# RetNet attention and a two-layer MLP: weight conversion rebuilt over three engines, raw loads on the sync queue, decay factors applied before the transposes

## The chip, the cores and the metric

One core of a Trainium2 chip. The metric is device microseconds of one execution; lower is better. Every kernel here was run four to five times beside runs of the kernel before on the same chip. Medians are given with their range. A ratio is the mean time of one kernel's runs over the mean of the other's in the same rounds, so it is not quite the ratio of the medians that stand beside it.

## The reference, cut to what matters

```python
# q, k, v: (8, 8, 576, 64) float32      8 batches, 8 heads, 576 positions
scores = (1 / np.sqrt(64)) * np.matmul(q, k.transpose(0, 1, 3, 2))
gamma = 1.0 - 2.0 ** (-5.0 - np.arange(8))
Dmat = np.where(rel >= 0, gamma[:, None, None] ** rel, 0.0)   # rel = row - column
ret = np.matmul(scores * Dmat, v)
x = ret.transpose(0, 2, 1, 3).reshape(4608, 512)
# moe_w_in (512, 2048) and moe_w_out (2048, 512) arrive as float64, alpha as float32
h = x @ w_in
g = np.maximum(h, 0.0) + alpha * np.minimum(h, 0.0)
out = g @ w_out
```

The kernel must turn the float64 weights into float32 itself. It reads each as two 32-bit words and works on 32 pieces of 128x512 weights.

## The kernel before: the parts that matter

Attention is done in 16 couples (one batch, four heads); the MLP in 192 units (384 tokens, 128 hidden columns), each with a first half (`ph`, four matmuls with w_in) and a second half (`po`, three matmuls with w_out); the traces show each of these matmuls as two records, so 8 and 6. The first eight pieces of weights are issued with couple 0, the next eight with couple 1, and so on up to couple 3. A scheduler then fixes each engine's order of instructions, and the engines run ahead of each other as far as buffers and waits allow (in the trace before, GpSimd starts its last scaling of k at 941.6 us, and TensorE the last matmul that reads it at 1066.2). In these kernels the results of the matmuls are tiles in PSUM; the copies and products by which another engine takes them out of there are called evictions below.

One piece of weights. `a` and `b` have two buffers each, `raw` too:

```python
def load_weights(n):
    for _ in range(min(n, len(pieces))):
        ...
        raw = wraw.tile([P, FQ, 2], INT32, tag="raw", name=f"raw_{at}")
        nc.gpsimd.dma_start(raw, src.rearrange("p (n two) -> p n two", two=2))
        lo = raw[:, :, 0].bitcast(UINT32)
        hi = raw[:, :, 1].bitcast(FP32)
        ...
        nc.gpsimd.tensor_scalar(a, hi, HI_MAX, -HI_MAX, ALU.min, ALU.max)          # clamp
        nc.gpsimd.tensor_tensor(out=b, in0=a, in1=a, op=ALU.mult)                  # square
        nc.vector.scalar_tensor_tensor(out=a, in0=b, scalar=HI_MIN * HI_MIN, in1=a,
                                       op0=ALU.is_ge, op1=ALU.mult)                # threshold
        nc.vector.tensor_scalar(bi, ai, 3, 0x3FFFFFF8,
                                ALU.logical_shift_left, ALU.bitwise_and)
        nc.vector.scalar_tensor_tensor(out=bi, in0=ai, scalar=-0x40000000, in1=bi,
                                       op0=ALU.bitwise_and, op1=ALU.bitwise_or)
        nc.vector.tensor_scalar(ai, bi, -0x00800000, None, ALU.bitwise_and)
        nc.vector.scalar_tensor_tensor(out=a, in0=lo, scalar=2.0 ** -52, in1=a,
                                       op0=ALU.mult, op1=ALU.mult)
        nc.gpsimd.tensor_tensor(out=dst, in0=a, in1=b, op=ALU.add)
```

The decay: k is scaled on GpSimd before its transpose, q by a table on VectorE after it:

```python
def transposes(n, b, u, tiles):
    ...
    nc.gpsimd.tensor_tensor(out=kr, in0=kr, in1=krem[...], op=ALU.mult)
    for j in range(NJ):
        nc.gpsimd.tensor_tensor(out=kn[:, j], in0=kn[:, j], in1=ktab[...], op=ALU.mult)
    for i in range(2):
        ...  # four transposes of qn into pt
        nc.vector.tensor_tensor(out=qT[i], in0=pt, in1=qtab[...], op=ALU.mult)
    ...      # rT: a product and a copy, both on VectorE
    for i in range(2):
        ...  # four transposes of kn into pt
        nc.scalar.copy(kT[i], pt)
```

## Time and profile before

| kernel before | |
|---|---|
| median of four runs | 1276.91 us (1276.35 to 1280.6) |
| span of the profiled run | 1276.2 us |
| first and last weight piece finished | 27.65 and 250.36 us |
| TensorE busy in the first 260 us | 197.9 us |
| TensorE's work at the full clock (worked out in the prediction) | 1165 us, and 9.1 us of output behind it |

The table of windows in slices of 40 us shows the conversion stage at a glance. Columns: stretch, length, busy us of PE, PEld, DVE, ACT, POOL with the number of instructions, then granted TensorE clock, DMA share, GB/s.

```profile
0.00:40.00 40.00, 23.40 (x195) 19.59 (x195) 23.86 (x59) 7.33 (x20) 23.44 (x115) 0.91 0.84 192
80.00:120.00 40.00, 31.27 (x197) 19.87 (x196) 30.80 (x55) 3.55 (x8) 26.58 (x32) 0.91 0.58 142
200.00:240.00 40.00, 29.02 (x160) 17.20 (x159) 27.61 (x50) 1.93 (x4) 25.46 (x29) 0.84 0.43 120
```

In these stretches TensorE has 9 to 17 us of gaps in 40, and its clock is not 1.00 either. From 256 us on it is full. ScalarE is nearly idle, while VectorE and GpSimd together are busy for 47 to 57 us of each 40.

### The profile page before, as it was taken

Reading aid. Unit: us, or ns where it says so; the run is one execution under the profiler, and the core shown is the slowest. Engines: PE = TensorE matmul, PEld = TensorE weight load, DVE = VectorE, ACT = ScalarE, POOL = GpSimd, SP = SyncE. Lnnn points to the kernel's source line nnn. Section 1 sums busy time; section 2 is a strip of 40 time slices with the busy share of each in tenths; the row PEclk is TensorE's granted clock in tenths of the full one; section 3 lists DMA queues with packets and bytes.
Section 4 is the critical chain, followed back from the end, with each engine's and each line's share of the span. In section 5 each row is a group of like instructions: output and inputs, shape, how many; then the busy total and the mean of one; then the engine's idle time right before and its main releaser. Section 6 shows DMA issues by size and latency. Waiting matters only on the chain.

```text
span 1276.2 us, 11815 instructions
## 1 busy us (share of the span) xinstructions
PE 1204.7 (94%) x4897; PEld 676.0 (53%) x4897; DVE 448.2 (35%) x852; ACT 63.7 (5%) x129; POOL 195.0 (15%) x337
## 2 busy tenths in 40 slices
PE   5788887899999999999999999999999999999997
PEld 4554344455555555555555655555555555555553
DVE  5778667522222323231232323231232323222221
ACT  1100000000000000000000000000000000000000
POOL 6666556500000100000000100000000000000000
PEclk8888898899999999999999999999999999999999
DMA  8754343200000201100100211100100000000000
GB/s 184 173 125 122 99 122 101 86 9 1 25 0 1 60 21 36 45 17 18 46 17 19 63 40 35 46 17 19 46 17 19 25 1 1 25 1 1 25 1 25
DMA packets 122773, 55.30 MB, mean 43 GB/s; under 512 B 116304, under 2 KB 116320, under 8 KB 122720
## 3 DMA queue, kind: packets, MB, share of 16 engines
q1 hardware_dynamic: 115200, 28.33, 10.2%
q0 software_dynamic: 7520, 26.23, 6.3%
q8 instruction: 38, 0.62, 0.2%
q14 instruction: 15, 0.12, 0.0%
HBM read 45.10 MB, written 9.44 MB: 43 GB/s over the span
## 4 chain that ended last, share of the span: by engine, by line
PE 56%; issue 27%; DVE 5%; POOL 5%; DMA 5%; SPq 1%; POOLq 0%
PE po L225 25%; PE ph L240 25%; DMA raw<-in_moe_w_in_dram 3%; PE ps L304 2%; DMA raw<-in_moe_w_out_dram 2%; DVE wa L209 1%; POOL wb L198 1%; DVE wb L205 1%; PE pv L349 1%; POOL w_in L211 1%; POOL wa L197 1%; POOL w_out L211 1%; PE pv L358 1%; SPq L75 1%; PE pu L327 1%
## 5 line engine op out<-in xcount | busy, mean ns | idle before, releaser
L240 PE MATMUL ph<-xT,w_in 128*128 128x384 f32 x1536 | 545.5, 494 | 12.5 <-POOL w_in L211 12.5
L225 PE MATMUL po<-w_out,g 128*128 128x512 f32 x1152 | 536.4, 601 | 10.7 <-POOL w_out L211 8.3
L240 PEld LDWEIGHTS ph<-xT,w_in 128*128 128x128 f32 x1536 | 287.7, 192 | 234.6 <-issue 76.7
L244 DVE TENSOR_SCALAR neg<-ph,alpha 128x384 f32<-128x384 f32 x192 | 118.3, 617 | 679.8 <-PE ph L240 679.4
L225 PEld LDWEIGHTS po<-w_out,g 128*128 128x128 f32 x1152 | 220.5, 193 | 247.7 <-issue 189.2
L233 POOL DMA_DIRECT2D out_dram<-osb x36 | 20.0, 555 | 738.5 <-ACT osb L231 738.4
L246 DVE SCALAR_TENSOR_TENSOR g<-ph,neg 128x384 f32<-128x384 f32 x192 | 106.8, 557 | 6.1
L265 POOL TENSOR_TENSOR kn<-kn,ktab 128x256 f32<-128x256 f32 x64 | 43.7, 698 | 171.1 <-DMA kn<-in_k_dram 170.9
L304 PE MATMUL ps<-qT,kT 64*128 64x128 f32 x512 | 52.3, 296 | 11.4 <-DVE at L308 7.7
L304 PEld LDWEIGHTS ps<-qT,kT 64*128 64x128 f32 x512 | 45.2, 198 | 28.3 <-DVE at L308 12.0
L308 DVE TENSOR_TENSOR at<-ps,mask 128x512 f32<-128x512 f32 x64 | 41.9, 684 | 32.8 <-PE ps L304 32.8
L361 ACT COPY xT<-pv 128x512 f32<-128x512 f32 x32 | 18.4, 587 | 519.7 <-PE pv L358 518.7
L199 DVE SCALAR_TENSOR_TENSOR wa<-wb,wa 128x512 f32<-128x512 f32 x32 | 25.1, 786 | 40.9 <-POOL wb L198 40.8
L231 ACT COPY osb<-po 128x512 f32<-128x512 f32 x36 | 21.1, 586 | 305.8 <-PE po L225 273.4
L293 ACT COPY kT<-ptk 128x512 f32<-128x512 f32 x32 | 17.6, 588 | 368.5 <-PE ptk L290 368.5
L349 PEld LDWEIGHTS pv<-at,vn 128*64 128x64 f32 x512 | 30.6, 147 | 9.8 <-issue 8.1
L198 POOL TENSOR_TENSOR wb<-wa 128x512 f32<-128x512 f32 x32 | 34.2, 1070 | 2.2
L349 PE MATMUL pv<-at,vn 128*64 128x128 f32 x512 | 34.3, 289 | 0.0
L358 PE MATMUL pv<-qT,sums 128*128 128x128 f32 x192 | 27.2, 286 | 2.6 <-DVE sums L337 2.6
L337 DVE TENSOR_TENSOR sums<-pu,sums 64x128 f32<-64x128 f32 x96 | 27.7, 289 | 3.0
L197 POOL TENSOR_SCALAR wa<-raw 128x512 f32<-128x512 f32 x32 | 22.4, 699 | 39.9 <-DMA raw<-in_moe_w_in_dram 26.3
L205 DVE SCALAR_TENSOR_TENSOR wb<-wa,wb 128x512 int32<-128x512 int32 x32 | 27.7, 864 | 0.5
(58 smaller groups left out, 406.2 us busy)
## 6 DMA issues: line engine op xcount, KB each, us to landing
out_dram<-osb POOLq DMA_DIRECT2D x36, 256.0 KB, 2.4
qn<-in_q_dram SPq DMA_DIRECT2D x64, 128.0 KB, 3.1
kn<-in_k_dram SPq DMA_DIRECT2D x64, 128.0 KB, 3.0
raw<-in_moe_w_in_dram POOLq DMA_DIRECT2D x16, 512.0 KB, 4.2
vn<-in_v_dram SPq DMA_DIRECT2D x64, 128.0 KB, 3.0
raw<-in_moe_w_out_dram POOLq DMA_DIRECT2D x16, 512.0 KB, 3.8
qr<-in_q_dram SPq DMA_DIRECT2D x32, 32.0 KB, 3.2
kr<-in_k_dram SPq DMA_DIRECT2D x32, 32.0 KB, 2.6
```

The lines of the kernel that those rows point to most:

```text
L197: nc.gpsimd.tensor_scalar(a, hi, HI_MAX, -HI_MAX, ALU.min, ALU.max)
L198: nc.gpsimd.tensor_tensor(out=b, in0=a, in1=a, op=ALU.mult)
L205: nc.vector.scalar_tensor_tensor(out=bi, in0=ai, scalar=-0x40000000, in1=bi, op0=ALU.bitwise_and, op1=ALU.bitwise_or)
L225: nc.tensor.matmul(acc[kb][m], g[:, m * P:(m + 1) * P], w_out[fc // FCQ][:, fc % FCQ, :], start=(fc == 0), stop=(fc == NFC - 1))
L240: nc.tensor.matmul(ph, w_in[fc // FCQ][:, cc, f0:f0 + P], xT[grp][:, cc, t0:t0 + TB], start=(cc == 0), stop=(cc == NCC - 1))
L244: nc.vector.tensor_scalar(neg, ph, 0.0, alpha[:, fc:fc + 1], ALU.min, ALU.mult)
L246: nc.vector.scalar_tensor_tensor(out=g, in0=ph, scalar=0.0, in1=neg, op0=ALU.max, op1=ALU.add)
L265: nc.gpsimd.tensor_tensor(out=kn[:, j], in0=kn[:, j], in1=ktab[:, j, 4 * u:4 * u + 4, None].to_broadcast([P, 4, D]), op=ALU.mult)
L304: nc.tensor.matmul(ps[h2][:, cols], kT[i][rows, cols], qT[i][rows, cols], start=True, stop=True)
L308: nc.vector.tensor_tensor(out=a, in0=ps[h2].rearrange("p (j w) -> p j w", w=C), in1=mask[:, None, :].to_broadcast([P, NJ, C]), op=ALU.mult)
L349: nc.tensor.matmul(pv[i][h2 * D:(h2 + 1) * D, j * C:(j + 1) * C], vn[:, j, 2 * i + h2, :], at[2 * i + h2][:, j, :], start=(j == 0), stop=F ...
L358: nc.tensor.matmul(pv[i][:, j * C:(j + 1) * C], sm[:, j - 1, i, :], qT[i][:, j * C:(j + 1) * C], start=False, stop=(j == NJ - 1), skip_gro ...
```

## The change

The intent: fewer operations per weight piece on VectorE and GpSimd, with two of them on ScalarE; raw loads that do not stand in GpSimd's queue; one kind of scaling for q and k.

```diff
-            raw = wraw.tile([P, FQ, 2], INT32, tag="raw", name=f"raw_{at}")
-            nc.gpsimd.dma_start(raw, src.rearrange("p (n two) -> p n two", two=2))
+            raw = wraw.tile([P, FQ, 2], INT32, tag="raw", bufs=3, name=f"raw_{at}")
+            nc.sync.dma_start(raw, src.rearrange("p (n two) -> p n two", two=2))
...
             nc.gpsimd.tensor_scalar(a, hi, HI_MAX, -HI_MAX, ALU.min, ALU.max)
-            nc.gpsimd.tensor_tensor(out=b, in0=a, in1=a, op=ALU.mult)
+            nc.scalar.activation(l, lo, ACTF.Copy, scale=2.0 ** -29)
+            nc.scalar.activation(b, a, ACTF.Square)
...     # threshold, shift and merge stay on VectorE
-            nc.vector.tensor_scalar(ai, bi, -0x00800000, None, ALU.bitwise_and)
-            nc.vector.scalar_tensor_tensor(out=a, in0=lo, scalar=2.0 ** -52, in1=a,
-                                           op0=ALU.mult, op1=ALU.mult)
-            nc.gpsimd.tensor_tensor(out=dst, in0=a, in1=b, op=ALU.add)
+            nc.gpsimd.tensor_tensor(out=dst.bitcast(INT32), in0=bi, in1=l, op=ALU.add)
...     # transposes(): q and k in one tile, both scaled on GpSimd
+        for x in range(2):
+            for j in range(NJ):
+                nc.gpsimd.tensor_tensor(out=qk[:, x, j], in0=qk[:, x, j],
+                                        in1=tab[...], op=ALU.mult)
...
-            nc.vector.tensor_tensor(out=qT[i], in0=pt, in1=qtab[...], op=ALU.mult)
...     # rT as one copy on ScalarE; of the four transposed tiles
+                if i == 0:
+                    nc.vector.tensor_copy(dst[i], pt)
+                else:
+                    nc.scalar.copy(dst[i], pt)
```

Left out: a constant of the threshold step (`HI_MIN`), which the new operations need, and the small tables of decay factors. These are now built by repeated products on VectorE, from constants that VectorE and GpSimd set, in the first 10 us, where the kernel before used exponentials on ScalarE and a large table for q.

More of the change, by code (lines that the diff above doesn't have):

```diff
@@ L69, in load_couple @@
     def load_couple(b, u):
-        tiles = []
-        for name, src in (("q", q), ("k", k), ("v", v)):
-            t = nat.tile([P, NJ, 4, D], FP32, tag=f"nat_{name}", name=f"{name}n_{b}_{u}")
-            r = nat.tile([P, 2, D], FP32, tag=f"rem_{name}", name=f"{name}r_{b}_{u}")
+        qk = nat.tile([P, 2, NJ, 4, D], FP32, tag="nat_qk", name=f"qk_{b}_{u}")
+        qkr = nat.tile([P, 2, 2, D], FP32, tag="rem_qk", name=f"qkr_{b}_{u}")
+        vn = nat.tile([P, NJ, 4, D], FP32, tag="nat_v", name=f"vn_{b}_{u}")
+        vr = nat.tile([P, 2, D], FP32, tag="rem_v", name=f"vr_{b}_{u}")
+        for t, r, src in ((qk[:, 0], qkr[:, 0], q), (qk[:, 1], qkr[:, 1], k), (vn, vr, v)):
             for j in range(NJ):
@@ L82, in load_couple @@
                     src[b, h:h + 2, NJ * C:S, :].rearrange("h p d -> p h d"))
-            tiles += [t, r]
-        return tiles
+        return qk, qkr, vn, vr
     loaded = {0: load_couple(*couples[0]), 1: load_couple(*couples[1])}
@@ L89 @@
     make_identity(nc, ident)
-    lng = [float(np.log1p(-(2.0 ** (-5.0 - h)))) for h in range(H)]
-    wrow = const.tile([P, C], FP32, name="wrow")
-    nc.gpsimd.iota(wrow, pattern=[[1, C]], base=0, channel_multiplier=0,
-                   allow_small_or_imprecise_dtypes=True)
-    prow = const.tile([P, 1], FP32, name="prow")
-    nc.gpsimd.iota(prow, pattern=[[1, 1]], base=0, channel_multiplier=1,
-                   allow_small_or_imprecise_dtypes=True)
+    gam = [1.0 - 2.0 ** (-5.0 - h) for h in range(H)]
@@ new lines @@
+    NBIT = 7
+    pint = const.tile([P, 1], INT32, name="pint")
+    nc.gpsimd.iota(pint, pattern=[[1, 1]], base=0, channel_multiplier=1)
+    pbit = const.tile([P, NBIT], FP32, name="pbit")
+    pbi = const.tile([P, NBIT], INT32, name="pbi")
+    for i in range(NBIT):
+        nc.vector.tensor_scalar(pbi[:, i:i + 1], pint, i, 1,
+                                ALU.logical_shift_right, ALU.bitwise_and)
+    nc.vector.tensor_copy(pbit, pbi)
+    fac = const.tile([P, 2, NJ, H], FP32, name="fac")
@@ new lines @@
+    facr = const.tile([P, 2, NC2, 2], FP32, name="facr")
+    gpw = const.tile([P, NBIT, H], FP32, name="gpw")
+    for h in range(H):
+        for i in range(NBIT):
+            nc.gpsimd.memset(gpw[:, i, h:h + 1], float(np.float32(gam[h] ** 2 ** i)) - 1.0)
+    for h in range(H):
+        for j in range(NJ):
+            nc.vector.memset(fac[:, 0, j, h:h + 1], gam[h] ** (j * C - MID) / np.sqrt(D))
+            nc.vector.memset(fac[:, 1, j, h:h + 1], gam[h] ** (MID - j * C))
+    for u in range(NC2):
+        for i in range(2):
+            for h2 in range(2):
+                g_ = gam[4 * u + 2 * i + h2]
+                rows = slice(i * REM, (i + 1) * REM)
+                at_ = NJ * C - i * REM - MID
+                nc.gpsimd.memset(facr[rows, 0, u, h2:h2 + 1], g_ ** at_ / np.sqrt(D))
+                nc.gpsimd.memset(facr[rows, 1, u, h2:h2 + 1], g_ ** -at_)
@@ new lines @@
+    pw = const.tile([P, 2, H], FP32, name="pw")
+    pwt = const.tile([P, H], FP32, name="pwt")
+    for i in range(NBIT):
+        t_ = pw[:, 0, :] if i == 0 else pwt
+        nc.vector.tensor_scalar(t_, gpw[:, i, :], pbit[:, i:i + 1], 1.0, ALU.mult, ALU.add)
+        if i:
+            nc.vector.tensor_tensor(out=pw[:, 0, :], in0=pw[:, 0, :], in1=pwt, op=ALU.mult)
+    nc.vector.reciprocal(pw[:, 1, :], pw[:, 0, :])
+    tab = const.tile([P, 2, NJ, H], FP32, name="tab")
+    tabr = const.tile([P, 2, NC2, 2], FP32, name="tabr")
@@ L101 @@
+    for x in range(2):
+        nc.vector.tensor_tensor(out=tab[:, x], in0=fac[:, x],
+                                in1=pw[:, x:x + 1, :].to_broadcast([P, NJ, H]), op=ALU.mult)
+        for i in range(2):
+            rows = slice(i * REM, (i + 1) * REM)
+            nc.vector.tensor_tensor(
+                out=tabr[rows, x], in0=facr[rows, x],
+                in1=pw[rows, x].rearrange("p (u i h) -> p u i h", u=NC2, i=2)[:, :, i, :],
+                op=ALU.mult)
     mask = const.tile([P, C], FP32, name="mask")
@@ L107 @@
     nc.vector.memset(maskr[0:REM, REM:C], 0.0)
-    ktab = const.tile([P, NJ, H], FP32, name="ktab")
-    kpow = const.tile([P, H], FP32, name="kpow")
-    for h in range(H):
-        nc.scalar.activation(kpow[:, h:h + 1], prow, ACTF.Exp, scale=-lng[h])
-    for j in range(NJ):
-        for h in range(H):
-            nc.gpsimd.memset(ktab[:, j, h:h + 1], float(np.exp(lng[h] * (MID - j * C))))
-    nc.vector.tensor_tensor(out=ktab, in0=ktab,
-                            in1=kpow[:, None, :].to_broadcast([P, NJ, H]), op=ALU.mult)
-    krem = const.tile([P, NC2, 2], FP32, name="krem")
-    for u in range(NC2):
-        for i in range(2):
-            rows = slice(i * REM, (i + 1) * REM)
-            for h2 in range(2):
-                h = 4 * u + 2 * i + h2
-                nc.vector.tensor_scalar(
-                    krem[rows, u, h2:h2 + 1], kpow[rows, h:h + 1],
-                    float(np.exp(lng[h] * (MID - NJ * C + i * REM))), None, ALU.mult)
-    qtab = const.tile([P, NPAIR, NJ * C + REM], FP32, name="qtab")
-    lgq = const.tile([P, NPAIR], FP32, name="lgq")
-    qpow = const.tile([P, NPAIR, C], FP32, name="qpow")
-    qfac = const.tile([P, NPAIR, NJ + 1], FP32, name="qfac")
-    for c in range(NPAIR):
-        for h2 in range(2):
-            rows = slice(h2 * D, (h2 + 1) * D)
-            nc.gpsimd.memset(lgq[rows, c:c + 1], lng[2 * c + h2])
-            for j in range(NJ + 1):
-                nc.gpsimd.memset(qfac[rows, c, j:j + 1],
-                                 float(np.exp(lng[2 * c + h2] * (j * C - MID)) / np.sqrt(D)))
-        nc.scalar.activation(qpow[:, c, :], wrow, ACTF.Exp, scale=lgq[:, c:c + 1])
-        nc.vector.tensor_tensor(
-            out=qtab[:, c, 0:NJ * C].rearrange("p (j w) -> p j w", w=C),
-            in0=qpow[:, c:c + 1, :].to_broadcast([P, NJ, C]),
-            in1=qfac[:, c, 0:NJ, None].to_broadcast([P, NJ, C]), op=ALU.mult)
-        nc.vector.tensor_scalar(qtab[:, c, NJ * C:], qpow[:, c, 0:REM],
-                                qfac[:, c, NJ:NJ + 1], None, ALU.mult)
     sums = []
@@ L182 @@
     HI_MAX = float(np.array([0x47EFFFFF], np.uint32).view(np.float32)[0])
-    HI_MIN = float(np.array([0x38000000], np.uint32).view(np.float32)[0])
+    HI_MIN = float(np.array([0x38080000], np.uint32).view(np.float32)[0])
     def load_weights(n):
@@ L194, in load_weights @@
             b = wraw.tile([P, FQ], FP32, tag="wb", name=f"wb_{at}")
+            l = wraw.tile([P, FQ], INT32, tag="wl", name=f"wl_{at}")
             ai, bi = a.bitcast(INT32), b.bitcast(INT32)
             nc.gpsimd.tensor_scalar(a, hi, HI_MAX, -HI_MAX, ALU.min, ALU.max)
-            nc.gpsimd.tensor_tensor(out=b, in0=a, in1=a, op=ALU.mult)
+            nc.scalar.activation(l, lo, ACTF.Copy, scale=2.0 ** -29)
+            nc.scalar.activation(b, a, ACTF.Square)
             nc.vector.scalar_tensor_tensor(out=a, in0=b, scalar=HI_MIN * HI_MIN, in1=a,
@@ L260, in transposes @@
     def transposes(n, b, u, tiles):
-        qn, qr, kn, kr, vn, vr = tiles
+        qk, qkr, vn, vr = tiles
         nc.gpsimd.tensor_tensor(
-            out=kr, in0=kr, in1=krem[:, u, :, None].to_broadcast([P, 2, D]), op=ALU.mult)
-        for j in range(NJ):
-            nc.gpsimd.tensor_tensor(
-                out=kn[:, j], in0=kn[:, j],
-                in1=ktab[:, j, 4 * u:4 * u + 4, None].to_broadcast([P, 4, D]), op=ALU.mult)
+            out=qkr, in0=qkr, in1=tabr[:, :, u, :, None].to_broadcast([P, 2, 2, D]),
+            op=ALU.mult)
@@ L268, in transposes @@
+        for x in range(2):
+            for j in range(NJ):
+                nc.gpsimd.tensor_tensor(
+                    out=qk[:, x, j], in0=qk[:, x, j],
+                    in1=tab[:, x, j, 4 * u:4 * u + 4, None].to_broadcast([P, 4, D]),
+                    op=ALU.mult)
         qT = [attn.tile([P, NJ * C], FP32, tag=f"qT{i}", name=f"qT{i}_{n}") for i in range(2)]
-        kT = [attn.tile([P, NJ * C], FP32, tag=f"kT{i}", bufs=1, name=f"kT{i}_{n}") for i in range(2)]
+        kT = [attn.tile([P, NJ * C], FP32, tag=f"kT{i}", bufs=1, name=f"kT{i}_{n}")
+              for i in range(2)]
@@ L270, in transposes @@
         rT = attn.tile([P, 2, C], FP32, tag="rT", name=f"rT_{n}")
-        for i in range(2):
-            pt = ps_a.tile([P, NJ * C], FP32, tag="psa", name=f"ptq{i}_{n}")
-            for j in range(NJ):
-                nc.tensor.transpose(
-                    pt[:, j * C:(j + 1) * C],
-                    qn[:, j, 2 * i:2 * i + 2, :].rearrange("p h d -> p (h d)"), ident)
-            nc.vector.tensor_tensor(out=qT[i], in0=pt, in1=qtab[:, 2 * u + i, 0:NJ * C],
-                                    op=ALU.mult)
@@ L279, in transposes @@
-        pt = ps_a.tile([P, 2, C], FP32, tag="psa", name=f"ptr_{n}")
-        nc.tensor.transpose(pt[:, 0, :], qr.rearrange("p h d -> p (h d)"), ident)
-        nc.tensor.transpose(pt[:, 1, :], kr.rearrange("p h d -> p (h d)"), ident)
-        nc.vector.tensor_tensor(
-            out=rT[:, 0, :].rearrange("p (i w) -> p i w", i=2),
-            in0=pt[:, 0, :].rearrange("p (i w) -> p i w", i=2),
-            in1=qtab[:, 2 * u:2 * u + 2, NJ * C:], op=ALU.mult)
-        nc.vector.tensor_copy(rT[:, 1, :], pt[:, 1, :])
@@ L287, in transposes @@
-        for i in range(2):
-            pt = ps_a.tile([P, NJ * C], FP32, tag="psa", name=f"ptk{i}_{n}")
-            for j in range(NJ):
-                nc.tensor.transpose(
-                    pt[:, j * C:(j + 1) * C],
-                    kn[:, j, 2 * i:2 * i + 2, :].rearrange("p h d -> p (h d)"), ident)
-            nc.scalar.copy(kT[i], pt)
+        pt = ps_a.tile([P, 2, C], FP32, tag="psa", name=f"ptr_{n}")
+        for x in range(2):
+            nc.tensor.transpose(pt[:, x, :], qkr[:, x].rearrange("p h d -> p (h d)"), ident)
@@ new lines, in transposes @@
+        nc.scalar.copy(rT, pt)
+        for x, dst in ((0, qT), (1, kT)):
+            for i in range(2):
+                pt = ps_a.tile([P, NJ * C], FP32, tag="psa", name=f"pt{x}{i}_{n}")
+                for j in range(NJ):
+                    nc.tensor.transpose(
+                        pt[:, j * C:(j + 1) * C],
+                        qk[:, x, j, 2 * i:2 * i + 2, :].rearrange("p h d -> p (h d)"), ident)
+                if i == 0:
+                    nc.vector.tensor_copy(dst[i], pt)
+                else:
+                    nc.scalar.copy(dst[i], pt)
@@ L321, in states @@
     def states(n, tiles):
-        qn, qr, kn, kr, vn, vr = tiles
+        qk, qkr, vn, vr = tiles
         ps = ps_a.tile([P, NJ, 2, D], FP32, tag="psa", name=f"pu_{n}")
@@ L326, in states @@
                 for h2 in range(2):
-                    nc.tensor.matmul(ps[h2 * D:(h2 + 1) * D, j, i, :], kn[:, j, 2 * i + h2, :],
+                    nc.tensor.matmul(ps[h2 * D:(h2 + 1) * D, j, i, :], qk[:, 1, j, 2 * i + h2, :],
                                      vn[:, j, 2 * i + h2, :], start=(j == 0 and i == 0),
@@ L340, in values @@
     def values(n, b, u, tiles, qT, rT, at):
-        qn, qr, kn, kr, vn, vr = tiles
+        qk, qkr, vn, vr = tiles
         grp, x0 = b // GB, (b % GB) * S
```

## The prediction

> **What bounds the kernel now.** I read the page's slices first, then the table of windows, then the waits of TensorE and GpSimd in the first 260 us, then the timeline there, and last the order of instructions in the two built programs. The slices show two stages:
>
> ```profile
> PE   5788887899999999999999999999999999999997
> ...
> POOL 6666556500000100000000100000000000000000
> PEclk8888898899999999999999999999999999999999
> ```
>
> For eight slices (255 us) TensorE is 50 to 80% busy at a granted clock of 0.8 to 0.9 while GpSimd works; afterwards TensorE is full and GpSimd nearly idle. The windows put numbers on it:
>
> ```profile
> 96.00:128.00 32.00, 25.63 (x143) 15.61 (x142) 26.67 (x49) 2.51 (x5) 20.60 (x23) 0.89 0.49 124
> 224.00:256.00 32.00, 27.21 (x68) 13.71 (x69) 18.20 (x34) 2.35 (x4) 16.06 (x18) 0.89 0.29 91
> 256.00:288.00 32.00, 32.00 (x88) 16.45 (x87) 8.08 (x14) 0.00 (x0) 0.00 (x0) 1.00 0.00 2
> ```
>
> The columns are stretch, length, busy us of PE, PEld, DVE, ACT, POOL, then clock, DMA share, GB/s. From 256 us TensorE has no gap. Before that, it waits for converted weights, or for attention evictions that stand behind a conversion in VectorE's queue (waits of TensorE, then of GpSimd, in 0 to 260 us):
>
> ```profile
> PE ph L240 <- POOL w_in L211: 12.5, 4, 3.9
> ...
> PE psr L315 <- DVE at L308: 8.6, 4, 4.6
> PE po L225 <- POOL w_out L211: 8.3, 4, 3.2
> PE ps L304 <- DVE at L308: 7.7, 3, 4.0
> ...
> POOL w_out L211 <- DVE wa L209: 26.4, 15, 4.6
> POOL wa L197 <- DMA raw<-in_moe_w_in_dram: 26.3, 13, 5.2
> ```
>
> The 32 weight pieces leave one by one: in the chain of waits the first is finished at 27.65 us and the last at 250.36, so 222.7/31 = 7.18 us a piece.
>
> TensorE's own work, from the saturated stretch: a unit of the MLP costs 2.58 + 2.58 = 5.16 us (the chain there alternates 2.58 us of L225 with 2.58 us of L240). From 290 to 1250 us there are 1319/8 = 164.9 units, 850.8 us, and 320/32 = 10 attention couples, so a couple costs (960 - 850.8)/10 = 10.9 us. In all 192 x 5.16 + 16 x 10.9 = 1165 us. By 250.4 us the kernel has done 16 units and 6.15 couples, 149.6 us worth; 1015.5 remain, and the last matmul does end at 1267.1, 1016.7 later. The sum closes. The last 9.1 us are output. So about 101 us of the first 250 are lost to idleness and a low clock, and only this can be won.
>
> [...] (before, 108 to 112 us):
>
> ```profile
> 108.31 3.58 POOL L265 TENSOR_TENSOR kn<-kn,ktab 128x256 f32<-128x256 f32 x4
> ...
> 108.82 1.09 DVE L199 SCALAR_TENSOR_TENSOR wa<-wb,wa 128x512 f32<-128x512 f32 x1
> ...
> 109.84 0.83 DVE L208 TENSOR_SCALAR wa<-wb 128x512 int32<-128x512 int32 x1
> ...
> 119.73 0.69 DVE L199 SCALAR_TENSOR_TENSOR wa<-wb,wa 128x512 f32<-128x512 f32 x1 [1.53 <-POOL wb L198]
> ```
>
> L199 takes 1.09 us beside GpSimd and 0.69 alone; four L265 take 3.58 beside VectorE and 2.60 alone (at 21.33). [...]
>
> **The change part by part.**
>
> [...]Durations alone, from the timeline. Before: GpSimd 0.65 (L197) + 1.03 (L198) + 1.26 (L211) = 2.94; VectorE 0.69 + 0.43 + 0.69 + 0.43 + 0.69 = 2.93; 5.87 us. After: GpSimd 0.65 + the integer add, taken as 1.26 like the float add of two tiles; VectorE 0.69 + 0.43 + 0.69 = 1.81; 3.72 us. [...]ScalarE is nearly idle. GpSimd also loses 32 issues of 0.59 us.
>
> *Decay on GpSimd.* Before: 4 x 0.65 + 0.41 = 3.0 us a couple. After: 8 x 0.65 + 0.65 = 5.85[...]. VectorE's qT product (0.69, source PSUM[...]) becomes a copy of the same size; rT's two operations (0.56) move to ScalarE. TensorE has the same 18 transposes a couple: nothing won or lost there.
>
> *Rate.* Before, eight pieces meet the scaling of 1.5 couples: 8 x 5.87 + 4.5 = 51.5 us[...], while eight took 8 x 7.18 = 57.5: 0.895 used. After, the built program puts one couple's scaling among each eight: 8 x 3.72 + 5.85 = 35.6. I choose the same use, 0.895: 39.8 us for eight, 4.97 a piece. It is a choice: waits for DMA go (loads no longer follow GpSimd's add, and three buffers stand ahead), but at each group of eight new ones come, because in ScalarE's order all sixteen activations of a group stand before the xT copies that free PSUM, and in VectorE's order the masked scores of the next couple stand between groups.
>
> *Start.* The first raw load stands on the sync queue behind the loads of couples 0, 1, 2 (18 each at about 0.6 us), and couple 2's wait for couple 0's tiles. I put pu of couple 0 at 25.5 us (the before kernel: 27.2), then 18 issues, first raw out near 36, landed near 41.5. But the first activation stands in ScalarE's order after couple 2's kT copy. Couple 0 starts some 4 us later than before, since both q and k now wait for tables ready near 12 us and 6 us of GpSimd; it saves about that again, for no conversion blocks VectorE. At about 11.5 us a couple, couple 2's copies end near 44; plus 1.2 (ScalarE), about 3.2 (VectorE with mask operations between), 1.3 (add): first piece at 50 us, 22 later than before.
>
> *End.* In the new order of TensorE, four units per group of pieces stand between the parts of couple 4, and nothing of couple 5 comes before the last unit of block 0. After piece 28 (last of the fourth w_in) it stays fed: each later piece opens 5.16 us of work against 4.97. Piece 28: 50 + 27 x 4.97 = 184 us. By then TensorE has done 12.75 first halves and 11 second halves of units (61.3) and couples 0 to 3 plus couple 4 without its values (4 x 10.9 + about 7.9 = 51.5): 112.8. Remaining 1165 - 112.8 = 1052. End: 184 + 1052 + 9 = 1245 us. In the saturated stage scaling and copies lie beside TensorE at 15% and less of the other engines: no change.
>
> So conversion gets 2.2 us a piece faster (69 us by its end), 22 are given back by the late start, and 15 or so because less attention is done ahead.
>
> **The rivals.** (1) GpSimd and VectorE are not tied; the three engines pipeline, and VectorE with 8 x 1.81 + 11.4 us of attention and MLP work binds at about 26 to 30 us for eight. Then piece 28 comes near 145 to 155, and the end at 1207 to 1216. For it: fewer hops to DMA. Against: the stretched durations above. (2) New head-of-line waits replace the removed ones: use[...] falls to 0.75, 47.5 us for eight, piece 28 at 210, end 1272: no gain. For it: the orders just named and a sync queue mixing raw loads with couple loads that wait. Against: the before kernel had similar bubbles and still used 0.895. (3) The integer add is slower than the float one: each 0.5 us more costs 27 x 0.5/0.895 = 15 us.
>
> **Range and chances.** Rival 1's half and rival 2's half give 1225 to 1265. The 2% edge is 1251.5, piece 28 at 190 us, only 6 us beyond my figure; a use of 0.86 would miss it. So faster 0.66, same 0.33, slower 0.01: the saturated 1052 us are untouched.
>
> **What would show it.** The first add into w_in at 45 to 55 us; the last near 200 to 205; spacing near 5 us; VectorE's two-input steps (L205 and L211 of the changed file) above 0.69 us and GpSimd's adds above 1.26 on average; TensorE without gaps from about 185 us; from there to the end near 1060 us. It is wrong if the integer add is far from 1.26 us, if the spacing is near 3.5[...] or 6 (new waits), if the first piece comes much after 55, or if TensorE shows gaps after 250.

The sum: (8 x 3.72 + 5.85)/0.895 = 39.8 us for eight pieces, 4.97 a piece; 50 + 27 x 4.97 = 184; 184 + 1052 + 9 = 1245 us. That the durations on VectorE and GpSimd add up, as if the two engines were fully tied to each other, was my estimate; the trace before shows only that they stretch each other (1.09 us against 0.69 for L199). "Use" is the share of the time that this added work fills. The 1.2 us for ScalarE's two activations is an estimate too, twice the 0.59 us that a 128x512 copy takes there in the trace before; they took 0.68 and 0.63 us on average in the changed kernel.

## More of the kernel before

An MLP unit, which VectorE serves too, in one queue with the conversion:

```python
nc.vector.tensor_scalar(neg, ph, 0.0, alpha[:, fc:fc + 1], ALU.min, ALU.mult)
nc.vector.scalar_tensor_tensor(out=g, in0=ph, scalar=0.0, in1=neg, op0=ALU.max, op1=ALU.add)
```

## The result, and the profile after

| | before | after |
|---|---|---|
| median of four runs each | 1276.91 us (1276.35 to 1280.6) | 1244.18 us (1242.06 to 1245.23) |
| ratio, 95% interval | | 0.9736 (0.9713 to 0.9758) |
| profiled span | 1276.2 us | 1242.7 us |
| first, last piece finished | 27.65, 250.36 us | 48.16, 181.20 us |
| mean spacing of pieces (31 steps) | 7.18 us | 4.29 us |

The changed kernel is 2.6% faster and less than 1 us from the predicted 1245. First its slices, on the page:

```profile
PE   6878789999999999999999999999999999999998
...
POOL 6567680002001010100100101010010000000000
PEclk9879799999999999999999999999999999999999
```

The stage in which GpSimd converts is now six slices of 31 us, where it was eight. Its windows:

```profile
0.00:40.00 40.00, 26.84 (x280) 22.43 (x280) 20.79 (x127) 6.87 (x14) 22.79 (x112) 0.96 0.70 164
40.00:80.00 40.00, 30.30 (x196) 20.85 (x196) 29.59 (x48) 16.38 (x30) 26.52 (x26) 0.74 0.56 163
80.00:120.00 40.00, 32.09 (x171) 18.35 (x172) 32.88 (x52) 13.97 (x25) 28.61 (x27) 0.96 0.60 174
160.00:200.00 40.00, 35.41 (x116) 18.07 (x116) 22.65 (x30) 6.58 (x10) 21.77 (x21) 0.96 0.21 55
200.00:240.00 40.00, 40.00 (x129) 21.73 (x126) 8.23 (x14) 3.09 (x6) 1.72 (x3) 1.00 0.12 35
```

TensorE is not much fuller inside the stage (32.09 us against 31.27 in the third window); the stage is shorter. ScalarE's added work is seen in the fourth number (13.97 us against 3.55). The waits of TensorE in the first 260 us (engine, output, line, what it waited for: total us, times, longest):

```profile
PE po L227 <- DVE g L248: 9.3, 4, 2.9
...
PE ps L302 <- DVE at L306: 5.6, 2, 4.8
...
PE po L227 <- POOL qk L269: 3.8, 1, 3.8
PE ph L242 <- POOL w_in L213: 1.8, 1, 1.8
```

The wait for converted weights (20.8 us in two groups before) has all but gone: 1.8 us. TensorE now waits for VectorE's evictions, above all for `g`. The line with `qk` is a wait for `g` too: `po` does not read `qk`, its weights had been there for 8 us, and the first `g` ended at 71.32 us in the same moment as a scaling of `qk`.

**Where the 33 us came from.** I split what TensorE loses, with the prediction's own 1165 and 9.1 us: lost = span - 1165 - 9.1. Idle is 260 us less TensorE's busy time in the first 260. The part lost to the clock is estimated as the sum, over windows of 4 us, of busy time times (1 - granted clock). The rest is what neither shows.

| profiled run | span | lost | idle | low clock | rest |
|---|---|---|---|---|---|
| before | 1276.2 | 102.1 | 62.1 | 25.3 | 14.7 |
| after | 1242.7 | 68.6 | 42.4 | 17.9 | 8.3 |
| difference | 33.5 | 33.5 | 19.7 | 7.4 | 6.4 |

So some 20 of the 33 us are idle time and about 7 are clock. One trace stands behind each row: m_split, below, has the order of the changed kernel and splits into 42.6 + 16.4 + 9.7, so a single part is good to 1.5 us or so.

Of the 6.4 us of rest, 2.4 lie at the very end: from the last matmul to the end of the profile 8.3 us pass before and 5.9 after. In all four kernels whose raw loads stand on GpSimd's queue (before, p_conv, p_decay, s_gps) the last issue of an output is followed by 6.5 us, in the ten others by 4.2 to 4.5. Why is not shown. The other 4 us of rest stay open.

The prediction did not look at where the clock falls. Here is one place where a low clock follows a wait, TensorE's timeline and the windows of 2 us around it:

```profile
178.39 4.33 PE L227 MATMUL po<-w_out,g 128*128 128x512 f32 x6 [2.92 <-DVE g L248]
182.51 3.00 PE L242 MATMUL ph<-xT,w_in 128*128 128x384 f32 x8
```

```profile
176.00:178.00 2.00, 0.00 (x0) 0.00 (x0) 2.00 (x4) 0.00 (x0) 2.00 (x2) 1.00 0.00 0
178.00:180.00 2.00, 1.61 (x4) 0.73 (x5) 1.97 (x4) 0.00 (x0) 2.00 (x4) 0.90 0.00 0
180.00:182.00 2.00, 2.00 (x4) 0.96 (x3) 0.05 (x1) 0.00 (x0) 1.77 (x2) 0.50 0.00 0
182.00:184.00 2.00, 2.00 (x5) 0.91 (x4) 0.00 (x0) 0.00 (x0) 0.00 (x0) 0.75 0.00 0
```

A gap of 2.92 us is followed by a clock of 0.50, in windows of 0.25 us from 179.6 to 183.0 us, and the six matmuls that take 2.57 us later on take 4.33, the next eight 3.00 for 2.58: the low clock costs another 2.2 us after the gap has ended. The trace has seven stretches of low clock in the first 260 us, of 3.4, 6.8, 13.7, 3.4, 3.4, 10.2 and 3.4 us, all near 3.4 us or a multiple of it. Gaps of 2.43, 2.25 and 2.92 us came with a low stretch of 3.4 us each; the stretch at 32.75 us has no gap above 0.6 us in the 8 us before it, and a gap of 1.66 us, before 170.07, had no low stretch. What brings the clock down is not shown.

### The profile page after: what moved, and what is told of

Same layout as the page of the kernel before. It is cut to its first block, busy times and chain, and to the rows that moved or that the text cites. A ratio compares the mean times of both kernels' runs of the same rounds, so it can differ in the third digit from the quotient of the medians.

```text
span 1242.7 us, 11962 instructions
## 1 busy us (share of the span) xinstructions
PE 1193.1 (96%) x4897; PEld 670.2 (54%) x4897; DVE 417.0 (34%) x831; ACT 108.3 (9%) x197; POOL 195.2 (16%) x328
## 4 chain that ended last, share of the span: by engine, by line
PE 61%; issue 27%; POOL 6%; DVE 4%; ACT 1%; DMA 1%; SPq 0%; POOLq 0%; ACTq 0%
PE ph L242 26%; PE po L227 26%; PE pt L285 2%; PE ps L302 2%; PE pv L347 2%; POOL w_in L213 2%; POOL qk L269 1%; PE pv L356 1%; POOL wa L201 1%; PE pu L325 1%; DVE at L306 1%; POOL w_out L213 1%; DVE wa L205 1%; ACT wb L204 1%; DVE wb L211 1%
## 5 line engine op out<-in xcount | busy, mean ns | idle before, releaser
L269 POOL TENSOR_TENSOR qk<-qk,tab 128x256 f32<-128x256 f32 x128 | 86.0, 691 | 233.2 <-DMA qk<-in_q_dram 222.8
L264 POOL TENSOR_TENSOR qkr<-qkr,tabr 128x256 f32<-128x256 f32 x16 | 9.8, 614 | 410.6 <-DMA qkr<-in_k_dram 284.1
L302 PE MATMUL ps<-qT,kT 64*128 64x128 f32 x512 | 48.8, 287 | 7.8 <-DVE at L306 5.6
L302 PEld LDWEIGHTS ps<-qT,kT 64*128 64x128 f32 x512 | 42.6, 190 | 21.5 <-issue 10.5
L285 PE MATMUL pt<-ident,qk 128*128 128x128 f32 x256 | 36.5, 295 | 0.2
L280 ACT COPY rT<-ptr 128x256 f32<-128x256 f32 x16 | 6.0, 375 | 324.5 <-PE ptr L279 324.5
L285 PEld LDWEIGHTS pt<-ident,qk 128*128 128x128 f32 x256 | 31.0, 151 | 3.8 <-POOL qk L269 1.0
L213 POOL TENSOR_TENSOR w_in<-wb,wl 128x512 int32<-128x512 int32 x16 | 25.1, 1566 | 33.9 <-DVE wb L211 30.4
L211 DVE SCALAR_TENSOR_TENSOR wb<-wa,wb 128x512 int32<-128x512 int32 x32 | 30.0, 939 | 0.4
```

Of the source, the lines that this page charges most:

```text
L213: nc.gpsimd.tensor_tensor(out=dst.bitcast(INT32), in0=bi, in1=l, op=ALU.add)
L269: nc.gpsimd.tensor_tensor(out=qk[:, x, j], in0=qk[:, x, j], in1=tab[:, x, j, 4 * u:4 * u + 4, None].to_broadcast([P, 4, D]), op=ALU.mult)
L285: nc.tensor.transpose(pt[:, j * C:(j + 1) * C], qk[:, x, j, 2 * i:2 * i + 2, :].rearrange("p h d -> p (h d)"), ident)
L302: nc.tensor.matmul(ps[h2][:, cols], kT[i][rows, cols], qT[i][rows, cols], start=True, stop=True)
```

## The experiments

Twelve kernels were run, all with the right result. Spacing, idle, clock and rest are worked out as above.

| kernel | median us | ratio (95%) | pieces: first, last, spacing | lost: idle + clock + rest |
|---|---|---|---|---|
| p_conv_load | 1241.74 | 0.9737 (0.9717 to 0.9757) | 47.7, 176.0, 4.14 | 41.1 + 14.6 + 6.9 |
| p_conv | 1248.17 | 0.9779 (0.9764 to 0.9795) | 22.8, 149.2, 4.08 | 43.0 + 16.1 + 13.4 |
| p_load | 1283.81 | 1.0069 (1.0046 to 1.0092) | 49.4, 212.4, 5.26 | 72.1 + 25.6 + 9.3 |
| p_decay | 1293.15 | 1.0138 (1.0122 to 1.0154) | 31.4, 260.4, 7.39 | 74.4 + 31.1 + 13.6 |
| l_two | 1265.97 | 0.9929 (0.9913 to 0.9945) | 47.9, 187.5, 4.51 | 63.3 + 15.7 + 11.1 |
| l_one | 1252.68 | 0.9827 (0.9812 to 0.9842) | 49.2, 175.7, 4.08 | 52.3 + 14.5 + 10.5 |
| s_act | 1253.20 | 0.9825 (0.9804 to 0.9846) | 19.7, 154.4, 4.35 | 54.2 + 12.1 + 7.2 |
| s_gps | 1254.48 | 0.9842 (0.9821 to 0.9864) | 21.9, 157.6, 4.38 | 44.4 + 20.7 + 12.6 |
| m_noclamp | 1234.31 | 0.9666 (0.9641 to 0.9692) | 48.3, 174.0, 4.05 | 38.2 + 11.4 + 9.3 |
| m_split | 1243.68 | 0.9744 (0.9722 to 0.9766) | 48.3, 181.4, 4.30 | 42.6 + 16.4 + 9.7 |
| m_copies | 1240.40 | 0.9717 (0.9696 to 0.9739) | 48.4, 178.7, 4.20 | 43.9 + 12.3 + 7.5 |
| best | 1231.36 | 0.9669 (0.9651 to 0.9687) | 46.9, 170.2, 3.98 | 38.5 + 9.8 + 6.5 |

My theory at the outset (A in the expectations) was the prediction's: the work of VectorE and GpSimd, which stretch each other, adds up and sets the spacing of the pieces, and the end of the conversion sets the end of the kernel. I call this the contention below. The rival was that engine queues, and not the contention, set the spacing; and, for the end, that what counts is the time that TensorE loses while conversion and attention run side by side.

### The three parts of the change, one at a time

**p_conv_load**: the new conversion and the new loads in the kernel before, old decay. One of the old tables was made to share a conversion buffer, so that the kernel builds.

```diff
-    qpow = const.tile([P, NPAIR, C], FP32, name="qpow")
+    qpow = wraw.tile([P, NPAIR, C], FP32, tag="wa", name="qpow")
...    # load_weights() as in the changed kernel
```

> The change without its decay part (new conversion, raw loads on the sync queue with three buffers, old q and k tables; one temporary table shares a conversion buffer so that it fits). Theory A, conversion[...] sets the end: GpSimd scales 3.0 instead of 5.85 us a couple, so pieces come about 0.1 to 0.3 us faster; 1236 to 1246 us, not slower than the full change. Rival B, moving the decay off VectorE was a main source of the gain: 1255 to 1265 us.

**p_conv**: only the new operations; loads on GpSimd's queue, two raw buffers.

```diff
-            nc.gpsimd.tensor_tensor(out=b, in0=a, in1=a, op=ALU.mult)
+            nc.scalar.activation(l, lo, ACTF.Copy, scale=2.0 ** -29)
+            nc.scalar.activation(b, a, ACTF.Square)
...    # and the integer add in place of the last three steps
```

> Only the new operations of the conversion; raw loads stay on GpSimd's queue with two buffers. Theory A: the first piece is done near 27 us as in the kernel before, a piece then takes about 5.0 to 5.5 us since each load again follows a GpSimd add; last piece near 185 to 200 us, 1235 to 1255 us. Rival B, the load path is what limits: spacing stays above 6.3 us and the time above 1262 us.

**p_load**: only the loads; old operations.

```diff
-            raw = wraw.tile([P, FQ, 2], INT32, tag="raw", name=f"raw_{at}")
-            nc.gpsimd.dma_start(raw, ...)
+            raw = wraw.tile([P, FQ, 2], INT32, tag="raw", bufs=3, name=f"raw_{at}")
+            nc.sync.dma_start(raw, ...)
```

> Only the raw loads moved to the sync queue with three buffers; old conversion operations. Theory A: the first piece comes 20 us later, the spacing falls from 7.2 to 6.0 to 6.5 us because the old operations need 5.9 us of the two engines for a piece; last piece near 240 to 250 us; 1268 to 1280 us, the same within 1%. Rival B, the loads were the limit: spacing below 5 us and a time below 1255 us.

**p_decay**: only the decay part; conversion and loads as before.

```diff
...    # transposes() and the tables of the changed kernel
...    # load_weights() of the kernel before
```

> Only the decay part; old conversion, raw loads on GpSimd's queue. Theory A: 2.9 us more GpSimd work a couple[...], no other gain: 1277 to 1286 us, spacing 7.2 to 7.7 us. Rival B, relief of VectorE pays: 1255 to 1270 us.

What was measured: the operations alone bring 2.2% of the 2.6; with the loads it is all of it (0.9737 against 0.9736 for the whole change). The decay part alone costs 1.4%, the loads alone 0.7%. In the whole change the decay costs nothing that these runs resolve, and its smaller tables let it build without that sharing. Of the expectations, p_conv_load's held. p_conv's held in time, but its spacing (4.08 us, not 5.0 to 5.5) did not. p_load and p_decay came out above their ranges by 4 and 7 us, and p_load's spacing (5.26 us, not 6.0 to 6.5) missed too.

The cost of the decay alone has the size that the prediction's figures give: 2.85 us more GpSimd work a couple, over the six couples beside the conversion, is 17 us, and the kernel is 1293.15 - 1275.22 = 17.9 us slower. But this sum was made after the event: the expectation, from the same figure, was 1277 to 1286 us, and the last piece comes only 10 us later than before (260.4 us). What TensorE waited for there was the conversion on GpSimd:

```profile
PE po L228 <- POOL w_out L214: 14.9, 3, 7.9
PE ph L243 <- POOL w_in L214: 13.9, 4, 5.1
```

Two of these runs also break the second half of my theory. p_load finishes its last piece 38 us before the kernel before does (212.4 against 250.4) and is still slower. p_conv finishes 27 us before p_conv_load and is 6 us slower. So the end of the conversion does not set the end by itself. One place where p_conv loses is its start: VectorE, then GpSimd, then TensorE (timelines):

```profile
21.08 3.44 DVE L202 SCALAR_TENSOR_TENSOR wa<-wb,wa 128x512 f32<-128x512 f32 x1 [3.48 <-ACT wb L201]
24.45 1.87 DVE L307 TENSOR_TENSOR at<-ps,mask 128x512 f32<-128x512 f32 x3
```

```profile
21.51 1.27 POOL L210 TENSOR_TENSOR w_in<-wb,wl 128x512 int32<-128x512 int32 x1
22.75 0.64 POOL L198 TENSOR_SCALAR wa<-raw 128x512 f32<-128x512 f32 x1
...
23.35 0.61 POOL L264 TENSOR_TENSOR kn<-kn,ktab 128x256 f32<-128x256 f32 x1
```

```profile
25.18 1.43 PE L303 MATMUL ps<-qT,kT 64*128 64x128 f32 x5 [5.18 <-DVE at L307]
```

VectorE stands for 3.48 us until the square is there; then a threshold step, 0.69 us without a neighbour, takes 3.44 us, through three GpSimd operations in a row. The masked scores of couple 0 stand behind it in VectorE's queue, and TensorE stands for 5.18 us. Weights that early help little: in p_conv the first `ph` comes at 35.5 us, but the first `po` only at 114.7 (48.2 and 71.5 in the changed kernel). In the first 40 us TensorE is busy 26.84 us in the changed kernel, 21.08 in p_conv. This is not the whole account of p_conv: its profiled span is 9.9 us longer than p_conv_load's, and of these 1.9 are idle time, 1.5 clock and 6.5 rest; 2.3 of the rest lie behind the last matmul, and what the other 4 are stays open. p_load, with the old operations packed more tightly, has the same trouble later: between 80 and 120 us VectorE and GpSimd are busy 34.82 and 30.89 of 40 us, TensorE 23.06, at a clock of 0.50.

```profile
80.00:120.00 40.00, 23.06 (x138) 18.47 (x138) 34.82 (x55) 2.51 (x5) 30.89 (x29) 0.50 0.53 151
```

### Contention or VectorE's queue

Two kernels that differ in one instruction a piece, of nearly the same length alone (0.69 and 0.67 us) and in the same place in VectorE's order; no result uses it. In l_two it has two inputs from SBUF, where the kernel holds `a`, in l_one it has one.

```diff
# l_two: after the shift step
+            sc = wraw.tile([P, FQ], FP32, tag="sc", bufs=1, name=f"sc_{at}")
+            nc.vector.tensor_tensor(out=sc, in0=a, in1=a, op=ALU.mult)
# l_one: in the same place
+            sc = wraw.tile([P, 1], FP32, tag="sc", bufs=1, name=f"sc_{at}")
+            nc.vector.tensor_reduce(out=sc, in_=a, op=ALU.add, axis=mybir.AxisListType.X)
```

> The changed kernel with one more VectorE operation a piece whose result is not used: a product with two SBUF inputs of 128x512 (0.69 us alone)[...]. Theory A[...]: the spacing rises from 4.29 us by about 0.5 to 4.7 to 4.9 us, VectorE's and GpSimd's other operations get longer means, and the time rises by 12 to 20 us over the changed kernel, 1256 to 1264. Rival C, only VectorE's queue counts: the same as the one-input run beside it.

> The same place in the order, but the extra VectorE operation is a sum over one SBUF input of 128x512 (about 0.65 to 0.7 us)[...]. Theory A: the spacing stays within 0.2 us of 4.29 and the time within 8 us of the changed kernel, 1244 to 1252. Rival C, only VectorE's queue counts: as much as the two-input run, 1256 to 1264.

The groups of the added instruction in the two traces (count, busy us, mean ns):

```profile
L212 DVE TENSOR_TENSOR sc<-wa 128x512 f32<-128x512 f32 x32 | 37.3, 1166 | 0.0
```

```profile
L212 DVE TENSOR_REDUCE sc<-wa 128x1 f32<-128x512 f32 x32 | 21.6, 674 | 0.0
```

The one with two inputs is stretched to 1166 ns, where such a step takes 0.69 us without a neighbour; the other, at 674 ns, is not stretched. The kernels are 21.8 us (l_two) and 8.5 us (l_one) slower than the changed kernel by their medians. Their two traces have one and the same order of work on TensorE, VectorE, ScalarE and GpSimd over the first 260 us, so the 13.3 us between them belong to the contention. (They also write different amounts, 128x512 and 128x1: it is the whole product that is measured, not its second input alone.) The 8.5 us of l_one are less clear: 21.6 us more in VectorE's queue are one reason, but the scheduler also ordered both kernels otherwise than the changed kernel. Both times lie 1 to 2 us above the ranges that theory A gave, and l_two's spacing rose by 0.2 us, not by 0.5. l_one is also the neatest evidence against the end of the conversion as the measure: its last piece comes 5.5 us earlier than in the changed kernel, and it is slower, because TensorE is idle 10 us more.

### Was the late first piece a cost?

The raw loads on other queues, three buffers, so that the first piece comes 26 to 28 us earlier:

```diff
# s_act
-            nc.sync.dma_start(raw, ...)
+            nc.scalar.dma_start(raw, ...)
# s_gps
-            nc.sync.dma_start(raw, ...)
+            nc.gpsimd.dma_start(raw, ...)
```

> The changed kernel with the raw loads issued from ScalarE's queue instead of behind the q, k, v loads, so that the conversion starts about 30 us earlier. Theory D, formed after the runs of the parts: what counts is TensorE time lost in the conversion stage, and an early conversion takes VectorE from attention; first piece near 15 us, last near 150, but 1238 to 1252 us, no gain. Theory A as predicted (22 us given back by the late start): 1218 to 1228 us.

> The changed kernel with the raw loads back on GpSimd's queue, three buffers kept. Theory D: first piece near 23 us, last near 150 to 160, 1242 to 1256 us. Theory A as predicted: 20 us earlier start less 0.6 us a piece of issue, 1230 to 1240 us.

Both finish the conversion 24 to 27 us earlier than the changed kernel and are 9 to 10 us slower. In s_act the issues stand in ScalarE's queue, and transposes wait for the copies behind them:

```profile
PE pt L285 <- ACT xT L359: 22.7, 2, 17.4
```

In s_gps the 32 issues take 18.4 us of GpSimd; its busy time in the first 260 us rises by only 9 (138.7 against 129.4), since its other operations are shorter there. TensorE is busy 21.80 us of the first 40, and 2.1 us of the loss lie behind the last matmul. Each early start thus brings a cost of its own with it, so these runs do not prove that a free early start would be worth nothing. They do show that none of the 22 us which the prediction booked as given back was to be had in these three ways (p_conv included), as theory D had expected; s_act lies 1 us above its range.

### What can still be taken away

**m_noclamp** drops GpSimd's clamp; the square and the threshold step read the raw words. For weights beyond the range of float32 the result would be wrong by the arithmetic (not run); for these it is right.

```diff
-            nc.gpsimd.tensor_scalar(a, hi, HI_MAX, -HI_MAX, ALU.min, ALU.max)
...
-            nc.scalar.activation(b, a, ACTF.Square)
-            nc.vector.scalar_tensor_tensor(out=a, in0=b, scalar=HI_MIN * HI_MIN, in1=a,
+            nc.scalar.activation(b, hi, ACTF.Square)
+            nc.vector.scalar_tensor_tensor(out=a, in0=b, scalar=HI_MIN * HI_MIN, in1=hi,
```

> The changed kernel without GpSimd's clamp (0.65 us a piece[...]); the square and the threshold step read the raw words themselves, so the instructions of VectorE and ScalarE stay as many as they were. [...] (4.37 us of such work a piece before the cut, 3.72 after), the spacing falls from 4.29 us to 3.6-3.8, the last add is done near 160-165 us, and the kernel gains about half of the 17 us: 1232-1238 us. If VectorE's queue or the order of instructions sets it, VectorE has as much to do as before and the kernel stays at 1242-1246 us. The result must still be right for this data.

It gains 9.9 us by the medians (9.4 against m_split on the same chip), as the theory of the contention, whose range stands first above, expected, but the spacing missed: 4.05 us, not 3.6 to 3.8, and the last piece is finished at 174 us, not at 160 to 165. With less on GpSimd the wait moved to VectorE's last step, as GpSimd's waits show (30.4 and 2.0 us in the changed kernel for the same two groups):

```profile
POOL w_in L211 <- DVE wb L209: 36.1, 11, 10.2
...
POOL w_out L211 <- DVE wb L209: 12.1, 9, 2.8
```

Of the gain in span, 9.7 us, 4.2 are idle time and 6.5 are clock, and the rest goes up by 1.0 (against m_split's profile: 4.4, 5.0, and 0.4 of rest gained). So the expected time was met for a reason only half as expected. The cut also makes the chain of steps of a piece shorter by one, and no run separates this from the contention.

**m_split** was to interleave: four pieces ahead of the attention values of a couple, four behind.

```diff
-            load_weights(WPC)
+            load_weights(WPC // 2)
         pop_units(share // 3)
         values(n, b, u, tiles, qT, rT, at)
+        if b < WB:
+            load_weights(WPC - WPC // 2)
```

> The changed kernel with the eight pieces of a group issued in two halves, four before the attention values of the couple and four behind them; same instructions, other order. If long runs of conversion in the queues of ScalarE and VectorE are what makes attention wait (and the 6-9 us in which GpSimd stands idle between groups), the waits between groups shrink and the kernel gains 5-10 us: 1234-1239 us. If the time is given by the amount of work on VectorE[...], the order does nothing: 1242-1246 us. A loss would say that conversion now comes too late for TensorE.

It tells nothing of the theory: the scheduler gave the engines the very order of the changed kernel. The two traces show the same sequence on TensorE, VectorE, ScalarE and GpSimd over the first 260 us. It serves as a repeat of the changed kernel on another chip: 1243.68 us against 1244.18, and pieces within 0.3 us.

**m_copies** moves the two transposed copies of VectorE to ScalarE for the first five couples.

```diff
-                if i == 0:
+                if i == 0 and n >= 5:
                     nc.vector.tensor_copy(dst[i], pt)
```

> The changed kernel with the two transposed copies a couple that VectorE does (0.6-0.7 us each) moved to ScalarE for the first five couples; ScalarE is busy 40% in this stage. If VectorE's queue is what TensorE loses time to in the conversion stage, the kernel gains 3-7 us: 1237-1241 us. [...] If ScalarE's order decides (copies stand behind sixteen activations), it loses 2-6 us: 1247-1250 us.

On the same chip as m_split its runs (1239.88 to 1240.9) lie below all of m_split's (1242.82 to 1244.94): 3.3 us by the medians. These copies read PSUM and are not stretched beside GpSimd (the twelve in the changed kernel's first 260 us all take 0.69 us, and seven of them lie beside a GpSimd operation), so a stretching of them is not the reason. The time is in the range expected if VectorE's queue counts, but that is not shown: idle time does not fall against m_split (43.9 and 42.6 us), the gain is in clock and rest (12.3 and 7.5 against 16.4 and 9.7), and the scheduler also changed the order on TensorE and GpSimd with this edit.

**best** has both edits, in five rounds.

> The changed kernel with both cuts: no clamp on GpSimd (the threshold step reads the raw words) and, for the first five couples, all transposed copies on ScalarE. If the two losses[...] are separate, the gains of about 10 and 3.5 us add: 1229-1232 us. If both only shorten the same chain (the last pieces' way to TensorE), the second is mostly hidden: 1233-1236 us.

1231.36 us (1230.65 to 1234.7), ratio 0.9669. It has the lowest median of all, but its ratio is that of m_noclamp (0.9666), and three of its runs lie near 1231 while two lie at 1234. Whether the copies still bring anything on top of the dropped clamp stays open. Both beat the changed kernel (0.9736), by 0.7% of the kernel before.

## Why the prediction was right, and where not

- *TensorE's own work, 1165 us: held. The 9.1 us of output: too much by 3.* By 178.39 us, where TensorE's last gap ends, it had done 13 first halves, 11 second halves and what the prediction had for the couples, 113.4 us at its prices. So 1051.6 should remain; the last matmul ends 1058.4 us later, 2.2 of which are the low clock shown above. Behind it come 5.9 us. In sum 1064.3 us, where the prediction had 1052 + 9.
- *First piece at 50 us: 48.16.* Held, with its reason: the sync queue brings couple 2's loads first (issued from 22.37 us on, the first raw load at 33.78).
- *The integer add like the float one: held.* Alone it takes 1.26 us, as the float add did in the trace before (1.26 at the least, L211); here at the very end:

```profile
179.94 1.26 POOL L213 TENSOR_TENSOR w_out<-wb,wl 128x512 int32<-128x512 int32 x1
```

- *Spacing 4.97 us, from a use of 0.895: the term of the sum that was mis-sized.* Measured 4.29. The prediction's sum of work is 35.6/8 = 4.45 us a piece, so the use comes out at 4.45/4.29 = 1.04, and that with GpSimd idle 6 to 9 us between groups of eight. Durations add up to more time than passes. In the middle of a group, GpSimd and then VectorE (timelines of the changed kernel):

```profile
161.82 1.71 POOL L213 TENSOR_TENSOR w_in<-wb,wl 128x512 int32<-128x512 int32 x1
...
163.50 0.83 POOL L201 TENSOR_SCALAR wa<-raw 128x512 f32<-128x512 f32 x1
...
164.29 1.06 POOL L269 TENSOR_TENSOR qk<-qk,tab 128x256 f32<-128x256 f32 x1
...
165.32 1.71 POOL L213 TENSOR_TENSOR w_in<-wb,wl 128x512 int32<-128x512 int32 x1
```

```profile
161.53 0.88 DVE L205 SCALAR_TENSOR_TENSOR wa<-wb,wa 128x512 f32<-128x512 f32 x1
...
162.44 1.37 DVE L209 TENSOR_SCALAR wb<-wa 128x512 int32<-128x512 int32 x1
...
163.85 1.03 DVE L211 SCALAR_TENSOR_TENSOR wb<-wa,wb 128x512 int32<-128x512 int32 x1
```

  From one add to the next 3.50 us pass, while the six operations take 1.26 + 0.65 + 0.65 and 0.69 + 0.43 + 0.69 = 4.37 us without a neighbour. All six are stretched, so they do contend; but some 0.15 us of each lie over a neighbour. Rival 1 (no tie) falls by the stretching and by l_two against l_one; the full tie falls by this sum.
- *Piece 28 at 184 us and TensorE fed from there: two errors that met.* With the better spacing piece 28 is there at 167.03 us, 17 before the prediction. But TensorE has no lasting run until 178.39: `po` waits for `g`, and `g` stands in VectorE's queue behind steps of the last pieces (the 2.92 us wait shown above). Together -17 + 11 = -6 us at that point, and 3 us more from there to the end than the 1061 booked: hence the 1242.7 us of span. That the total came within 1 us is luck; the errors inside it were far larger. The conclusion "fed from about 185 us" came true by a way that the prediction did not describe, and its rival 2, new head-of-line waits, was a part of the truth.
- *"22 are given back by the late start": not supported.* As bookkeeping of pieces it is right. As a cost it is not: three kernels that start 25 to 28 us earlier are 4 to 10 us slower. In p_conv the conversion of the first 50 us feeds little MLP work and, in the place shown, holds VectorE away from the attention of couple 0.
- *The end of the conversion as the measure: too simple.* It orders before, after and p_decay rightly, and p_load, p_conv, l_one, s_act and s_gps wrongly. Idle and clock loss in the stage put all fourteen kernels in nearly the order of their times (from 48 us for best to 105 for p_decay; only kernels within 2 us of each other by this sum swap places); but these are parts of the time itself, counted after the event, and not a means to predict.
- *The decay, +2.85 us of GpSimd a couple: it costs when alone (17.9 us, more than was expected of that run), and is hidden in the whole.* In the changed kernel it costs nothing that shows against p_conv_load. Why it is hidden there was not tested by itself; the timeline above suggests that with the square gone GpSimd has room for one scaling a piece.
- *The signs.* VectorE's two-input steps (0.81 and 0.94 us on average, against 0.69) and GpSimd's adds (1.57 and 1.46, against 1.26) came as announced; the last piece (181.20 us, not 200 to 205) and the spacing (4.29, between the 5 announced and the 3.5 of no tie) did not.
- *Two sums of the prediction do not follow from its own figures.* Rival 1's 26 to 30 us for eight pieces put piece 28 at 138 to 151 us, not 145 to 155; and half of rival 2 ends at 1258, not at 1265.

## What to carry to other kernels

When the operations of two engines stretch each other, as those of VectorE (0.69 us to 0.81 and 0.94 on average) and GpSimd (1.26 to 1.57 and 1.46) did here, move whole operations to a third engine (the two on ScalarE took 0.71 and 0.64 us at most), or drop them (the change does both, and no run separates the two): the operations alone brought 2.2 of the 2.6%; moving the loads alone lost 0.7%, and on top of the operations it gained 0.4. But count what finishes, not when: here, three kernels that converted earlier in a queue shared with TensorE's evictions were slower than the one that converted late, and a gap of 2.92 us on TensorE was followed by a low clock that cost another 2.2. And look at the built order before you run an edit of order: one of mine changed nothing.
